# Fused block-causal attention and a routed expert layer: moving the gate products, the routing steps and the scatters of the records within the attention slots

## The chip, the cores and the metric

The kernel runs on one core of a Trainium2 chip. The core has a matrix engine (TensorE, here PE; its weight loads are shown apart as PEld), VectorE (DVE), ScalarE (ACT), GpSimd (POOL) and SyncE (SP), which issues most DMA transfers. The metric is the device time of the one launch in microseconds (us), given as the median of several runs.

## What is computed

```python
# attention: q, k, v are [8, 8, 576, 64] float32
scores = scale * np.matmul(q, k.transpose(0, 1, 3, 2))        # scale = 1/8
scores = np.where(block_i >= block_j, scores, -1e9)           # blocks of 64
scores = scores - np.max(scores, axis=-1, keepdims=True)
attn = np.exp(scores)
attn = attn / (np.sum(attn, axis=-1, keepdims=True) + 1e-09)
attn_out = np.matmul(attn, v)

# routed layer: x is [4608, 512], one row a token
x = attn_out.transpose(0, 2, 1, 3).reshape(B * S, H * D)
logits = x @ w_gate + modality_bias[modality_id]              # 8 experts
e_idx = np.argmax(logits, axis=1)
gate_w = softmax(logits)[np.arange(N), e_idx]
for e in range(E):
    h = np.maximum(x[mask] @ w1[e], 0.0)                      # mask = (e_idx == e)
    out[mask] = gate_w[mask, None] * (h @ w2[e])              # inner width 1024
```

## The kernel before

**Tiling.** The 64 pairs of batch and head are taken two heads at a time: 32 pairs, four to a batch (`PPB`). One pair fills the 128 partitions, head 0 on the lower 64 and head 1 on the upper 64. The 576 positions are nine blocks of 64; block row s needs the scores against blocks 0 to s.

**Stages of a pair**, one letter each in the order table, and the engine:

- `Q` (POOL, line 203; `A` on ACT from pair 18 on) scales q in the tile `raw`, which `L` and `l` load over SP's queue. `v`, `v1`, `v2` load the values, `Y` loads `vt`, the values turned for the gates. A queue's transfers go in the order of issue, and a transfer waits for its buffer.
- `S0` to `S3`: the scores (PE, line 223, 40 matmul rows, shape 64\*64) into PSUM banks 0 to 5 (4 and 5 are one tile, `wide`).
- `M0` to `M4`: the maxima of the score rows (DVE, line 232), nine a pair; `E0` to `E4`: the exponentials (ACT) into `pm`, in the units of `UNITS`.
- `T0` to `T2`: transposes of 64 x 128 pieces of `pm` (PE, line 270, 16 + 16 + 14 pieces, two heads each; shape 64\*128), back into the same banks.
- `C0` to `C4`: copies of the transposed banks to `pt` (line 284). `ON_DVE` names those on DVE, here copy 1 alone; the rest are on ACT.
- `G`: the gate columns, v times the gate's weights (PE, line 290, 24 rows, shape 128\*64) into bank `b0` from column `GATES` on; `H` (ACT) copies them beside the values, so that the value product gives the logits of the gate along with the output.
- `V`: the value product (PE, line 312) into `o0` and `b0`: first 20 rows for the odd blocks (`TAILS`, 64 deep, shape 64\*64, the "short blocks"), then 80 rows, shape 128\*64 (`PRODUCTS`). [...]
- `D`, `Z0`, `Z1`: the reciprocal of the sums (DVE, lines 327 and 328) and the rows (DVE, lines 340 and 341): products and gate logits are divided into the token records `xr` and into `gl`. After these the banks `o0` and `b0` are free.

**Slots.** There is no loop on the chip: the program is laid out in 32 slots, and `run_slot` walks the table `ORDER` once per slot. Each entry is a stage and a distance: in slot n an entry with distance d works on pair n - d. So one slot loads pair n + 2, scores pair n + 1, transposes and copies pair n, and multiplies pair n - 1. The order is by hand; each engine works its instructions strictly in that order. The gates of pair n stand between its transposes and the scores of pair n + 1.

**Routing.** When the four pairs of a batch are through (`Z1` of pair 3, 7, ...), `routing` adds 20 small steps to a list: logits, total (PE, line 365), its copy out, bias, maximum, hits, index, first, one-hot, counts (PE, lines 406 and 408), shift, exponential, copy out of the counts, weight, running, and five that find the place of each token in its expert's list. The entries `q1` to `q6` of the order take up to 4 (`q1`) or 2 steps; total and counts are taken at `qp` only, their copies at `qv`. A batch's steps stretch over some three slots. The last one writes the indices `pi` (line 437) and queues nine **scatters** (line 440: an indirect DMA, issued by POOL, which writes the 128 records of a block row to their places in `records`, 77824 rows of 272 numbers in HBM). One scatter is issued at each of the spots `SPOTS` = V, T2, M1 of a slot.

**Experts.** From slot 19 on POOL also splits the first expert's weights into a high and a low part (lines 643 and 644, the step "prep" in `EARLY_STEPS`), loaded by the steps "stage". The last value product and the last scatters lie inside the first expert products (table `LAST`). Then two matmuls per token tile and expert run to the end of the program.

## Time and profile before

| | |
|---|---|
| runs | 707.65, 708.3, 709.89 us; median 708.3 |
| profiled execution | 709.1 us, of it the span of the trace 707.2 |
| PE | 688.3 us busy (97%), granted clock 0.996 over the span |
| PE weight loads | 577.6 us (82%) |
| DVE | 341.1 us (48%) |
| ACT | 327.4 us (46%) |
| POOL | 209.5 us (30%) |

A slot's start is where its first short block's product begins. Sums by stretch show one slot beside another, timelines show single instructions and, behind them in brackets, how long the engine had stood idle and what released it; "issue" means that the trace shows nothing for which it waited. Neighbouring instructions on PE overlap in such rows, so what a row of products takes is read from one start to the next, not from its duration.

### The profile page before, as it was taken

How to read it: one execution, taken by the hardware profiler on the slowest of the kernel's cores; microseconds unless marked ns; L12 is line 12 of the kernel's file. 1: busy time of each engine (PE TensorE's matmuls, PEld its weight loads, DVE VectorE, ACT ScalarE, POOL GpSimd, SP SyncE). 2: the span in 40 equal slices, each digit the busy share in tenths (PEclk: the TensorE clock that was granted, in tenths of full speed). 3: DMA queues.
4: the chain of work that ended last, by engine and by line, in shares of the span. 5: the costliest groups of instructions: out<-in, count | busy, mean ns of one | idle time of the engine just before them, and what ended most of it. 6: DMA issues, size and time to landing. Idle time of an engine off the chain costs nothing. (4 is left out here: it accounts for less than half of the span.)

```text
span 707.2 us, 21037 instructions
## 1 busy us (share of the span) xinstructions
PE 688.3 (97%) x8647; PEld 577.6 (82%) x8647; DVE 341.1 (48%) x929; ACT 327.4 (46%) x654; POOL 209.5 (30%) x246
## 2 busy tenths in 40 slices
PE   8999999989999999999999999999999999999996
PEld 5887887878788888888888888888888888888894
DVE  5786776868697878574132421424113142232121
ACT  6886776768787879432131321313113032231221
POOL 2424445250648583669012020301002010020201
PEclk9999999999999999999999999999999999999999
DMA  7555555565787787504842141501707031020100
GB/s 232 158 161 163 172 168 173 158 182 151 238 221 235 229 247 209 134 33 150 152 89 91 25 96 60 119 1 33 204 1 227 11 56 65 1 82 1 61 28 22
DMA packets 68451, 85.48 MB, mean 121 GB/s; under 512 B 12350, under 2 KB 54782, under 8 KB 68352
## 3 DMA queue, kind: packets, MB, share of 16 engines
q1 hardware_dynamic: 61824, 64.59, 34.7%
q0 software_dynamic: 6528, 19.50, 7.6%
q8 instruction: 69, 1.13, 0.7%
q14 instruction: 30, 0.25, 0.1%
HBM read 62.97 MB, written 21.27 MB: 119 GB/s over the span
## 5 line engine op out<-in xcount | busy, mean ns | idle before, releaser
L802 DVE SCALAR_TENSOR_TENSOR extra<-bank,extra 128x512 fp32r<-128x512 f32 (+1 forms) x70 | 46.8, 669 | 242.7 <-ACT extra L801 242.7
L801 ACT ACTIVATE extra<-bank 128x512 fp32r<-128x512 f32 (+1 forms) x70 | 40.6, 580 | 215.3 <-PE bank L798 215.3
L312 PE MATMUL b<-v,pt 64*64 64x73 f32 (+1 forms) x1612 | 103.4, 228 | 4.8 <-issue 4.7
L241 ACT ACTIVATE pm<-bank,nm 128x64 f32<-128x64 f32 (+3 forms) x192 | 88.0, 531 | 33.4 <-DVE nm L232 32.0
L232 DVE TENSOR_REDUCE nm<-bank 128x1 f32<-128x64 f32 (+3 forms) x192 | 80.6, 482 | 42.0 <-PE bank L223 32.3
L440 POOL DMA_INDIRECT records<-xr,pi x72 | 73.5, 1020 | 90.9 <-DVE pt L284 41.7
L312 PE MATMUL o<-v,pt 64*64 64x73 f32 (+1 forms) x1488 | 96.4, 230 | 2.3 <-issue 2.3
L312 PEld LDWEIGHTS o<-v,pt 64*64 64x64 f32 (+1 forms) x1488 | 82.1, 137 | 16.4 <-issue 11.0
L312 PEld LDWEIGHTS b<-v,pt 64*64 64x64 f32 (+1 forms) x1612 | 87.0, 137 | 7.1 <-issue 6.5
L223 PE MATMUL bank<-raw 64*64 64x448 f32 (+5 forms) x768 | 88.8, 441 | 0.0
L223 PE MATMUL wide<-raw 64*64 64x128 f32 (+3 forms) x512 | 59.9, 369 | 1.3 <-ACT pm L241 0.9
L284 ACT COPY pt<-bank 128x512 f32<-128x512 f32 x95 | 49.7, 594 | 20.5 <-PE bank L270 19.6
L798 PE MATMUL bank<-extra,w0ha 128*128 128x512 f32 (+1 forms) x176 | 59.2, 362 | 0.0
L798 PE MATMUL bank<-extra,w0la 128*128 128x512 f32 (+1 forms) x152 | 56.6, 372 | 0.0
L915 POOL DMA_INDIRECT out<-scratch,ids_b x9 | 8.8, 974 | 155.1 <-ACT scratch L914 154.2
L223 PEld LDWEIGHTS bank<-raw 64*64 64x64 f32 x768 | 40.9, 133 | 13.8 <-issue 6.9
L907 PE MATMUL late<-extra 128*128 128x512 f32 x216 | 50.4, 389 | 0.0
L798 PE MATMUL bank<-xtl,w0ha 128*128 128x512 f32 x128 | 49.8, 389 | 0.0
L798 PE MATMUL bank<-extra,w0hb 128*128 128x512 f32 x128 | 49.8, 389 | 0.0
L798 PE MATMUL bank<-extra,w0lb 128*128 128x512 f32 x128 | 49.8, 389 | 0.0
L798 PE MATMUL bank<-xtl,w0hb 128*128 128x512 f32 x128 | 49.8, 389 | 0.0
L241 ACT ACTIVATE pm<-wide,nm 128x128 f32<-128x128 f32 (+2 forms) x96 | 43.8, 526 | 10.8 <-DVE nm L232 8.1
(239 smaller groups left out, 1230.0 us busy)
## 6 DMA issues: line engine op xcount, KB each, us to landing
vt<-qk SPq DMA_DIRECT2D x32, 288.0 KB
v<-vr SPq DMA_DIRECT2D x62, 146.0 KB
xr<-records SPq DMA_DIRECT2D x32, 256.0 KB
raw<-qk SPq DMA_DIRECT2D x30, 240.0 KB
raw<-qk SPq DMA_DIRECT2D x30, 192.0 KB
raw<-qk SPq DMA_DIRECT2D x30, 144.0 KB
staging<-w SPq DMA_DIRECT2D x32, 128.0 KB
v<-vr SPq DMA_DIRECT2D x31, 73.0 KB
```

What stands on the lines that cost most here:

```text
L223: pe.matmul(place(s, a, b)[64 * t : 64 * t + 64], d.q[hs, D * s : D * s + D], d.k[hs, a:b], start=True, stop=True)
L232: dve.tensor_reduce(pairs[p].nm[:, s : s + 1], whole(s), AX.X, ALU.max, negate=True)
L241: act.activation(d.pm[:, o : o + D * (s + 1)], whole(s), AF.Exp, bias=d.nm[:, s : s + 1], scale=1.0)
L284: dve.tensor_copy(dst, src) if c in (ON_DVE if p else FIRST_ON_DVE) else act.copy(dst, src)
L312: pe.matmul(o, d.pt[rows, at, t : t + 64], d.v[rows, block, h, :], start=key not in begun, stop=last)
L440: last = pool.indirect_dma_start(records[:], bass.IndirectOffsetOnAxis(ap=g.pi[:, i : i + 1], axis=0), xr[:, i, :], None, bounds_check=2 * ...
L798: nc.tensor.matmul(hp, w[:, kc, ms], x[:, kc, 0:n], start=i == 0, stop=i == len(mm) - 1)
L801: nc.scalar.activation(hh, hp, AF.Relu)
L802: nc.vector.scalar_tensor_tensor(hl, hp, 0.0, hh, ALU.max, ALU.subtract)
L907: nc.tensor.matmul(y, s.hs[m][x][:, ts], self.part(w, 1, m // 2)[:, m % 2, :], start=first, stop=last)
L915: last = nc.gpsimd.indirect_dma_start(self.out, bass.IndirectOffsetOnAxis(ap=s.list.ids[:, s.t + i : s.t + i + 1], axis=0), yo, None, boun ...
```

## The change

- `V` is split: `tails` (V) multiplies the short blocks, `values` (W) the rest. Between them now stand the gates of the next pair (`G`) and the entry `qm`, at which total and counts are taken. Since the short blocks have by then started the banks, gates, total and counts no longer start them (`start` is false, but for pair 0 and the last batch).
- Order within the slot: the loads of `vt` (`Y`) come ahead of the values' (`v1`, `v2`); on DVE the copies come ahead of the rows `Z0`, `Z1`; transposes go T0, T2, T1, and blocks are regrouped among banks and transposes (`UNITS`, `GROUPS`, `ROOMS`, `PIECES`, `FLIP`) with the same number of rows. Slot 0 has an order of its own.
- Copy 2 is on DVE too, except for the last pair of a batch and for the six pairs of `BUSY`.
- `q9`, ahead of the scores and maxima, takes up to six routing steps in slots 13 and 29 (`QUICK`); the other entries take other numbers of steps.
- Scatters go at T2 and M1, at V too only in slots with slot % 4 == 1; in slots 30 and 31 at five spots.
- "stage1" and "restage" move from `qp` to `v1`, "ids" from slot 21 to 24, and the opening of pair 0 interleaves maxima and exponentials in another way.

```diff
...
-UNITS = ((7,), (5, 0), (4, 2), (6,), (3, 1, 8))
+UNITS = ((7,), (4, 2), (5, 0), (3, 1, 8), (6,))
...
-FLIP = (5, 0, 3, 1, 8)
-PIECES = (((7, 0, 512),), ((5, 0, 384), (0, 0, 64)), ((4, 0, 320), (3, 0, 256), (1, 0, 128), (2, 0, 192)), ((8, 512, 576), (8, 0, 512), (6, 0, 448)))
+FLIP = (4, 2, 3, 1, 8)
+PIECES = (((7, 0, 512),), ((4, 0, 320), (2, 0, 192)), ((8, 0, 512), (5, 0, 384), (0, 0, 64)), ((6, 0, 448), (8, 512, 576), (3, 0, 256), (1, 0, 128)))
...
-ON_DVE, FIRST_ON_DVE = (1,), (1, 3)
+ON_DVE, FEW_ON_DVE, FIRST_ON_DVE = (1, 2), (1,), (1, 2, 3)
+BUSY = (13, 14, 15, 16, 29, 30)
...
-ORDER = (
-    ("Q", -1), ("L", -2), ("V", 1), ("v", -1), ("l", -2), ("v1", -1), ("v2", -1), ("D", 1), ("Z0", 1), ("Z1", 1), ("q1", 1), ("T0", 0), ("C0", 0), ("C1", 0), ("T1", 0), ("C2", 0), ("C3", 0),
-    ("T2", 0), ("C4", 0), ("G", 0), ("H", 0), ("Y", -1), ("qp", 1), ("q2", 1), ("q3", 1), ("q4", 1), ("qv", 1), ("A", -2), ("S0", -1), ("S1", -1), ("S2", -1), ("S3", -1), ("M0", -1), ("E0", -1), ("M1", -1), ("E1", -1), ("M2", -1), ("E2", -1),
+BEGIN = (("Q", -1), ("L", -2), ("V", 1), ("G", 0), ("qm", 1), ("W", 1), ("v", -1), ("l", -2), ("Y", -1), ("v1", -1), ("v2", -1), ("D", 1), ("T0", 0), ("C0", 0))
+END = (
+    ("qp", 1), ("q2", 1), ("H", 0), ("qv", 1), ("q9", 1), ("A", -2), ("S0", -1), ("S1", -1), ("S2", -1), ("S3", -1), ("M0", -1), ("E0", -1), ("M1", -1), ("E1", -1), ("M2", -1), ("E2", -1),
     ("M3", -1), ("E3", -1), ("M4", -1), ("E4", -1), ("q5", 1), ("q6", 1),
 )
+FIRST_ORDER = (*BEGIN, ("C1", 0), ("T1", 0), ("C2", 0), ("C3", 0), ("T2", 0), ("C4", 0), *END)
+ORDER = (*BEGIN, ("C1", 0), ("T2", 0), ("C4", 0), ("T1", 0), ("C2", 0), ("C3", 0), ("Z0", 1), ("Z1", 1), ("q1", 1), *END)
...
-OPENING = (((0, 2, 1, 3), ((0,),)), ((6, 5, 4, 7), ((2,), (1, 3))), ((8,), ((5,), (6,), (4,), (7,), (8,))))
...
+OPENING = (("s", 0), ("p", 0, 2, 1, 3), ("m", 0), ("s", 1), ("m", 2), ("e", 0, 2), ("p", 5, 6, 4, 7), ("m", 1, 3), ("e", 1, 3), ("p", 8), ("m", 5), ("e", 5), ("m", 6), ("e", 6), ("m", 4), ("e", 4), ("m", 7), ("e", 7), ("m", 8), ("e", 8))
...
+SPOTS, LATE_SPOTS = ("V", "T2", "M1"), ("V", "T2", "S0", "M1", "M4")
 EARLY_STEPS = {
     **{(slot, name): ("prep",) for slot in range(19, 30) for name in SPOTS if (slot, name) != (29, "M1")},
-    (18, "V"): ("chosen",), (18, "qp"): ("stage",), (19, "qp"): ("stage1",), **{(slot, "qp"): ("restage",) for slot in range(20, 31)}, (31, "qp"): ("restage1",), **{(slot, "v2"): ("more",) for slot in range(19, 32)}, (21, "L"): ("ids",), (26, "T0"): ("fetch",), (31, "T0"): ("fetch",), (30, "S0"): ("turn0",), (31, "V"): ("low0", "low0"),
+    (18, "V"): ("chosen",), (18, "qp"): ("stage",), (19, "v1"): ("stage1",), **{(slot, "v1"): ("restage",) for slot in range(20, 31)}, (31, "v1"): ("restage1",), **{(slot, "v2"): ("more",) for slot in range(19, 32)}, (24, "L"): ("ids",), (26, "T0"): ("fetch",), (31, "T0"): ("fetch",), (30, "S0"): ("turn0",), (31, "V"): ("low0", "low0"),
...
...
-        dve.tensor_copy(dst, src) if c in (ON_DVE if p else FIRST_ON_DVE) else act.copy(dst, src)
+        dve.tensor_copy(dst, src) if c in (FIRST_ON_DVE if not p else FEW_ON_DVE if p % PPB == PPB - 1 or p in BUSY else ON_DVE) else act.copy(dst, src)
...
-                pe.matmul(b0[64 * c : 64 * c + 64, o : o + 2 * NE], vt[:, at : at + 64], wg[:, p % PPB, :], start=True, stop=True)
+                pe.matmul(b0[64 * c : 64 * c + 64, o : o + 2 * NE], vt[:, at : at + 64], wg[:, p % PPB, :], start=not p, stop=not p)
...
+    def product(p, s, block, at, rows, last):
+        d = pairs[p]
+        bank, c = column(p, s)
+        for h in range(2):
+            t = 64 * (h ^ (s in FLIP))
+            o = bank[t : t + 64, VW * c : VW * c + VW]
+            key = (s in SUMS[0], t)
+            pe.matmul(o, d.pt[rows, at, t : t + 64], d.v[rows, block, h, :], start=key not in d.begun, stop=last)
+            d.begun.add(key)
+
+    def tails(p):
+        pairs[p].begun = set()
+        for s, block, at, upper in TAILS:
+            product(p, s, block, at, slice(64 * upper, 64 * upper + 64), False)
+        assert len(pairs[p].begun) == 4
...
-        for s, block, at, upper in TAILS:
-            product(s, block, at, slice(64 * upper, 64 * upper + 64), False)
         for n, ((s,), j) in enumerate(PRODUCTS):
             side = SUMS[s not in SUMS[0]]
-            product(s, j, POS[s, j], slice(0, 128), all(x[0] not in side for x, _ in PRODUCTS[n + 1 :]))
+            product(p, s, j, POS[s, j], slice(0, 128), all(x[0] not in side for x, _ in PRODUCTS[n + 1 :]))
...
-                pe.matmul(tot[c], ii[:, c], g.l0, start=True, stop=True)
+                pe.matmul(tot[c], ii[:, c], g.l0, start=b == B - 1, stop=b == B - 1)
...
-                pe.matmul(ps[c, 0 : NSUB * NE].rearrange("p (e c) -> p c e", e=NE), ones[:, c], ohe.rearrange("p (c e) -> p c e", e=NE), start=True, stop=True)
+                pe.matmul(ps[c, 0 : NSUB * NE].rearrange("p (e c) -> p c e", e=NE), ones[:, c], ohe.rearrange("p (c e) -> p c e", e=NE), start=b == B - 1, stop=b == B - 1)
             for c in (slice(0, 64), slice(64, 128)):
-                pe.matmul(ps[c, NSUB * NE :], lead[:, c], ohe, start=True, stop=True)
+                pe.matmul(ps[c, NSUB * NE :], lead[:, c], ohe, start=b == B - 1, stop=b == B - 1)
...
-        total.kind = counts.kind = "qp"
+        total.kind = counts.kind = "qm"
...
     def run_slot(slot):
         nonlocal steps, ex
-        for name, stage in LAST if slot == NPAIR else ORDER:
+        for name, stage in LAST if slot == NPAIR else ORDER if slot else FIRST_ORDER:
             p = slot - stage
-            if placing and slot < NPAIR and name in SPOTS:
+            if placing and slot < NPAIR and name in (LATE_SPOTS if slot >= NPAIR - 2 else SPOTS[slot % PPB != 1 :]):
...
-                for _ in range(1 if kind else 4 if name == "q1" else 2):
+                chosen = steps and getattr(steps[0], "kind", "") == "c"
+                if kind:
+                    most = 1
+                elif name == "q9":
+                    most = 6 * (slot in QUICK)
+                elif name == "q1":
+                    most = 3 if chosen else 4
+                elif name == "q2":
+                    most = 2 * (not chosen)
+                else:
+                    most = 4 if chosen or slot % PPB == PPB - 1 or slot - 1 in QUICK else 2
+                for _ in range(most):
                     if slot > 1 and steps and getattr(steps[0], "kind", "") in kinds:
                         steps.pop(0)()
                 continue
```

**PE, a slot in which a batch's total is taken** (pair 7 multiplies, pair 8 is transposed; `cf` with `pm` is a transpose, `raw` a score, `wg` a gate, `l` the total, `v` with `pt` a value product). Before:

```order
L270 MATMUL bank_98<-cf,pm_111 128x64
L270 MATMUL wide<-cf,pm_111 128x64 x14
L290 MATMUL b_100<-wg,vt 64x16 x12
L365 MATMUL o_99<-l_886,cf 64x72 x2
L223 MATMUL bank_95<-raw_107 64x512 x2
L223 MATMUL bank_97<-raw_107 64x384 x2
```

After:

```order
L311 MATMUL b_100<-v_109,pt_113 64x73 x2
L311 MATMUL o_99<-v_109,pt_113 64x73 x2
L292 MATMUL b_100<-wg,vt 64x16 x12
L369 MATMUL o_99<-l_950,cf 64x72 x2
L311 MATMUL o_99<-v_109,pt_113 64x73 x2
L311 MATMUL b_100<-v_109,pt_113 64x73 x2
```

Gates and total stood between the last transposes and the first scores; now they stand between the short blocks (64x73, the first rows of `v` with `pt`) and the rest of the value product, whose rows the program names in the same way. Transposes are followed by scores.

**DVE, a slot with routing steps of batch 1**, from the reciprocal to the first maxima (`den`, `inv`: the reciprocal; COPY `pt`: copies 1 and 2; `xr`, `gl`: the rows; `ix`, `oh`: routing; `nm`: maxima). Before:


**DVE, the slot in which the one-hot of batch 0 is made** (`den`, `inv`: the reciprocal; COPY `pt`: copies 1 and 2; `xr`, `gl`: the rows; `ix`, `oh`, `df`: routing; `nm`: maxima). Before:

```order
L328 RECIPROCAL inv<-den 128x9
L340 TENSOR_TENSOR xr_79<-b_100,inv 128x5x64
L341 TENSOR_TENSOR gl<-b_100,inv 128x40
L340 TENSOR_TENSOR xr_79<-o_99,inv 128x4x64
L341 TENSOR_TENSOR gl<-o_99,inv 128x32
L397 TENSOR_REDUCE ix<-eq 128x9
L401 TENSOR_TENSOR oh<-cf,ix 128x72
L284 COPY pt_114<-bank_96 128x2x4x64
L384 TENSOR_TENSOR df<-lg,mx 128x72
L232 TENSOR_REDUCE nm<-bank_95 128x1
```

After:

```order
L332 RECIPROCAL inv<-den 128x9
L286 COPY pt_113<-bank_96 128x2x4x64
L286 COPY pt_113<-bank_97 128x8x64
L344 TENSOR_TENSOR xr_79<-b_100,inv 128x5x64
L345 TENSOR_TENSOR gl<-b_100,inv 128x40
L344 TENSOR_TENSOR xr_79<-o_99,inv 128x4x64
L345 TENSOR_TENSOR gl<-o_99,inv 128x32
L401 TENSOR_REDUCE ix<-eq 128x9
L405 TENSOR_TENSOR oh<-cf,ix 128x72
L236 TENSOR_REDUCE nm<-bank_95 128x1
L236 TENSOR_REDUCE nm<-bank_96 128x1 x2
```

The copies stand ahead of the rows, copy 2 is new on DVE, and the slot is the one before (its copies go to the other tile `pt`): the counts, which take `oh`, now come at `qm` of the next slot.

**POOL, the scatters of batch 0** (DMA `records`, x2 for two in a row; `raw`: the scale `Q`; `xr` from `cf`: the token numbers of the next batch). Before:

```order
L203 TENSOR_SCALAR raw_107<-raw_107 128x576
L440 DMA records<-xr_105,pi 77824x272 x2
L203 TENSOR_SCALAR raw_106<-raw_106 128x576
L440 DMA records<-xr_105,pi 77824x272 x3
L203 TENSOR_SCALAR raw_107<-raw_107 128x576
L440 DMA records<-xr_105,pi 77824x272
L354 TENSOR_SCALAR xr_79<-cf 128x9
L440 DMA records<-xr_105,pi 77824x272 x2
L203 TENSOR_SCALAR raw_106<-raw_106 128x576
L440 DMA records<-xr_105,pi 77824x272
L203 TENSOR_SCALAR raw_107<-raw_107 128x576
```

After:

```order
L207 TENSOR_SCALAR raw_107<-raw_107 128x576
L444 DMA records<-xr_105,pi 77824x272
L358 TENSOR_SCALAR xr_79<-cf 128x9
L444 DMA records<-xr_105,pi 77824x272
L207 TENSOR_SCALAR raw_106<-raw_106 128x576
L444 DMA records<-xr_105,pi 77824x272 x3
L207 TENSOR_SCALAR raw_107<-raw_107 128x576
L444 DMA records<-xr_105,pi 77824x272 x2
L207 TENSOR_SCALAR raw_106<-raw_106 128x576
L444 DMA records<-xr_105,pi 77824x272 x2
L207 TENSOR_SCALAR raw_107<-raw_107 128x576
```

Before, the nine stood as 2, 3, 1, 2, 1 between the scales; now the first comes a scale later and they stand as 1, 1, 3, 2, 2. Behind the last weight conversions, later in the queue, POOL now has five scatters of batch 5 and five of batch 6 in a row; before, five of batch 6 alone.

## Rows read from the trace of the kernel before

**Rows 1.** The page's first part: busy us (share of the span) xinstructions.

```profile
PE 688.3 (97%) x8647; PEld 577.6 (82%) x8647; DVE 341.1 (48%) x929; ACT 327.4 (46%) x654; POOL 209.5 (30%) x246
```

**Rows 2.** Sums by stretch: length, busy us (instructions) by engine, clock, DMA share, GB/s.

```profile
93.37:101.47 8.10, 8.10 (x215) 7.18 (x210) 7.30 (x28) 6.62 (x15) 1.38 (x2) 1.00 0.58 159
101.47:113.91 12.44, 10.61 (x215) 8.35 (x208) 5.34 (x16) 7.00 (x15) 10.28 (x10) 1.00 0.53 163
139.19:152.36 13.17, 11.10 (x214) 8.43 (x207) 7.22 (x34) 7.38 (x15) 11.22 (x11) 1.00 0.55 168
177.72:188.51 10.79, 9.59 (x214) 7.79 (x210) 6.19 (x19) 7.57 (x17) 7.63 (x11) 1.00 0.75 214
250.01:258.94 8.93, 8.73 (x215) 7.48 (x211) 5.92 (x19) 7.51 (x17) 7.95 (x12) 1.00 0.85 259
284.55:294.97 10.42, 8.71 (x174) 7.54 (x167) 6.26 (x18) 5.62 (x13) 6.14 (x6) 0.84 0.72 166
294.97:702.00 407.03, 406.88 (x1968) 339.15 (x1964) 123.11 (x231) 101.67 (x170) 73.51 (x79) 1.00 0.26 70
```

**Rows 3.** Timeline of PE around the gates: start us, us, instruction, shape, count, idle before.

```profile
90.00 0.88 PE L290 MATMUL b<-wg,vt 128*64 128x16 f32 x24
90.72 0.24 PE L406 MATMUL o<-oh,ones 128*64 128x72 bf16 x2
...
96.61 1.21 PE L270 MATMUL bank<-cf,pm 64*128 64x64 f32 x32
97.66 0.60 PE L270 MATMUL wide<-cf,pm 64*128 64x64 f32 x14
98.19 0.88 PE L290 MATMUL b<-wg,vt 128*64 128x16 f32 x24
99.00 0.65 PE L223 MATMUL bank<-raw 64*64 64x512 f32 x4
```

**Rows 4.** Timeline of PE in slot 11, beside the scatters of rows 5.

```profile
101.65 0.52 PE L312 MATMUL o<-v,pt 64*64 64x73 f32 x4
102.54 0.30 PE L312 MATMUL b<-v,pt 64*64 64x73 f32 x2 [0.37 <-issue]
...
105.09 0.57 PE L312 MATMUL b<-v,pt 128*64 128x73 f32 x4
106.02 0.44 PE L312 MATMUL b<-v,pt 128*64 128x73 f32 x5 [0.37 <-issue]
106.80 0.36 PE L312 MATMUL b<-v,pt 128*64 128x73 f32 x3 [0.34 <-issue]
107.53 0.36 PE L270 MATMUL bank<-cf,pm 64*128 64x64 f32 x5 [0.38 <-issue]
108.28 0.90 PE L270 MATMUL bank<-cf,pm 64*128 64x64 f32 x22 [0.38 <-issue]
```

**Rows 5.** Timeline of POOL, single scatters and a scale.

```profile
99.78 1.02 POOL L440 DMA_INDIRECT records<-xr,pi  x1 [8.64 <-DVE pt L284]
101.11 0.98 POOL L440 DMA_INDIRECT records<-xr,pi  x1 [0.30 <-issue]
...
118.57 1.66 POOL L203 TENSOR_SCALAR raw<-raw 128x576 f32<-128x576 f32 x1 [5.16 <-DMA raw<-qk]
...
282.36 1.00 POOL L440 DMA_INDIRECT records<-xr,pi  x1 [11.40 <-DVE pi L437]
...
288.03 1.47 POOL L440 DMA_INDIRECT records<-xr,pi  x1 [0.30 <-issue]
```

**Rows 6.** What gates (L290) and counts (L406) waited for: us, times.

```profile
  DVE gl L341: 1.9, 6
...
  DVE oh L401: 0.4, 1
```

**Rows 7.** Timeline of DVE: first and last of four row instructions, and the copy.

```profile
88.99 0.49 DVE L340 TENSOR_TENSOR xr<-b,inv 128x320 f32<-128x320 f32 x1
...
89.83 0.20 DVE L341 TENSOR_TENSOR gl<-o,inv 128x32 f32<-128x32 f32 x1
...
90.33 0.68 DVE L284 COPY pt<-bank 128x512 f32<-128x512 f32 x1
```

More of the change, by code (lines that the diff above doesn't have):

```diff
@@ L39 @@
 NWARM = 7
+QUICK = (13, 29)
 FIRST = 256
@@ L86 @@
 }
 LAST = (
-    ("+up0", 0), ("+place", 0), ("V", 1), ("+place", 0), ("D", 1), ("Z0", 1), ("Z1", 1), ("+steps1", 0), ("+place", 0), ("+up1", 0),
+    ("+up0", 0), ("+place", 0), ("V", 1), ("W", 1), ("+place", 0), ("D", 1), ("Z0", 1), ("Z1", 1), ("+steps1", 0), ("+place", 0), ("+up1", 0),
     ("+place", 0), ("+steps8", 0), ("+place", 0), ("+up2", 0), ("+place", 0), ("+steps11", 0), ("+up3", 0), ("+flush", 0),
@@ L243, in exps @@
     def exps(p, u):
-        for s in UNITS[u]:
+        for s in (8, 3, 1) if u == 3 else UNITS[u]:
             exp(p, s)
@@ L249, in opening @@
         pairs[0].nm = sml.tile([128, NSUB], F32, name="nm")
-        for n, (products, rows) in enumerate(OPENING):
-            if n < 2:
-                part = q[:, n * FIRST : FIRST if n == 0 else S]
-                dve.tensor_scalar(part, part, SCALE, None, ALU.mult)
-            for s in products:
-                for a, b in ((512, 576), (0, 512)) if s == 8 else ((0, D * (s + 1)),):
-                    score(0, s, a, b)
-            for together in rows:
-                for s in together:
-                    maximum(0, s)
-                for s in together:
-                    exp(0, s)
+        for what, *items in OPENING:
+            for s in items:
+                if what == "s":
+                    part = q[:, 0:FIRST] if s == 0 else q[:, FIRST:S]
+                    dve.tensor_scalar(part, part, SCALE, None, ALU.mult)
+                elif what == "p":
+                    for a, b in ((512, 576), (0, 512)) if s == 8 else ((0, D * (s + 1)),):
+                        score(0, s, a, b)
+                else:
+                    (maximum if what == "m" else exp)(0, s)
     def transposes(p, g):
@@ L300, in column @@
         return sides(p)[k], SUMS[k].index(s)
-    def values(p):
-        d = pairs[p]
-        begun = set()
-        def product(s, block, at, rows, last):
-            bank, c = column(p, s)
-            for h in range(2):
-                t = 64 * (h ^ (s in FLIP))
-                o = bank[t : t + 64, VW * c : VW * c + VW]
-                key = (s in SUMS[0], t)
-                pe.matmul(o, d.pt[rows, at, t : t + 64], d.v[rows, block, h, :], start=key not in begun, stop=last)
-                begun.add(key)
-        for s, block, at, upper in TAILS:
-            product(s, block, at, slice(64 * upper, 64 * upper + 64), False)
+    def product(p, s, block, at, rows, last):
[12 more added lines that the diff above has]
+        assert len(pairs[p].begun) == 4
+    def values(p):
         for n, ((s,), j) in enumerate(PRODUCTS):
             side = SUMS[s not in SUMS[0]]
-            product(s, j, POS[s, j], slice(0, 128), all(x[0] not in side for x, _ in PRODUCTS[n + 1 :]))
+            product(p, s, j, POS[s, j], slice(0, 128), all(x[0] not in side for x, _ in PRODUCTS[n + 1 :]))
     def inverse(p):
@@ L496, in emit @@
         one = {
-            "L": lambda: load(p), "Q": lambda: scale(p), "A": lambda: scale_late(p), "V": lambda: values(p), "D": lambda: inverse(p), "G": lambda: gates(p), "H": lambda: gates_out(p), "Y": lambda: load_turned(p),
+            "L": lambda: load(p), "Q": lambda: scale(p), "A": lambda: scale_late(p), "V": lambda: tails(p), "W": lambda: values(p), "D": lambda: inverse(p), "G": lambda: gates(p), "H": lambda: gates_out(p), "Y": lambda: load_turned(p),
             "v": lambda: load_blocks(p, 4, 6, slice(64, 128)), "l": lambda: load_part(p, QK_PARTS[2:]), "v1": lambda: load_blocks(p, 0, 2), "v2": lambda: load_blocks(p, 2, 4),
```

8 lines of the change are left out of this document (4 added, 4 removed), and 6 rows, old and new, of the table GROUPS.

## The prediction

> **What bounds the kernel now.** I read the page first, then the sums by stretch, then the timelines of TensorE (PE) and GpSimd (POOL). PE is busy 97% of the span and no other engine half of it [rows 1]; the last 407 us, the experts' products, are PE without a gap at full clock [rows 2]. Nothing in them is edited, so they move as a block, and the question is what the 32 attention slots take, 295 us. A slot is one pass over the order table. An undisturbed slot takes 8.10 us, and PE and its weight loads fill it [rows 2]. Others with the same 214 or 215 matmul rows take 12.44, 13.17, 10.79 and 8.93 us [rows 2]. I compared every slot's start with the next (the first products of the short blocks mark it): together the 31 slots lose about 31 us against the undisturbed one, and they lose it in three ways.
>
> First, **changes of the matmul's shape**. The gates stand between transposes (64*128) and scores (64*64), themselves 128*64. Followed by scores, 24 gate rows take 0.81 us (98.19 to 99.00); followed by counts of their own shape, 0.72 (90.00 to 90.72) [rows 3]. So gate to score costs 0.09. The last 14 transposes take 0.53 before a gate; at the pace of the 32 ahead of them (1.05, so 0.033 each) they would take 0.46: 0.07 more [rows 3].
>
> Second, **runs of scatters**. In slots 7, 8, 11, 12, 15, 16, 19 and 31 PE stands still with "issue" as the only releaser, each time while POOL issues scatters back to back, 1.0 us each and 0.3 apart [rows 4, 5]. Of two in a row whose first lies on scores, the second (101.11 [rows 5]) makes the four rows at 101.65 take 0.89 us to the next instead of some 0.1: 0.8 lost [rows 4]. For three in a row, the 17 rows from 105.09 to 108.28 should take 0.54 us at the 0.032 of a gate row or a transpose, and take 3.19: 2.65 lost [rows 4]. Four singles in a slot, with other POOL work between them, go with 8.93 instead of 8.10: 0.2 each [rows 2]. [...] Why PE is held I cannot say from these rows; that it is held I can.
>
> Third, **waits of the gates and counts for VectorE (DVE)**: 1.9 us in six slots for the logits of the pair before, 0.4 for the one-hot [rows 6].
>
> **The change, part by part.**
>
> *Gates, totals and counts move between the short blocks and the values' product.* No matmul goes. The shape change from short blocks to value products is there anyway; the gates now take it, and value products follow in the gates' own shape. Gone are the two changes around the old place, 0.09 + 0.07; new is the step from transposes straight to scores, which no row shows. Bounds: nothing, or the whole 0.16. The nearest rows are the two single changes, so 0.08. The gain is 0.08 x 31 = **2.5 us**, between 0 and 5.0. [...]
>
> *The gates' waits.* At the new place the gates write a bank that the short blocks ahead of them needed free already, and the counts' one-hot is made a slot earlier. Both waits go: **2.3 us**. What is late next is below.
>
> *Scatters.* The first scatter of a batch used to stand in POOL's queue behind one scale, some 9 us before its indices were ready (8.64 us idle at 99.78 [rows 5]), and the scale behind it came late, so three, then three more ran in a row. Now the last routing step ends a slot before the first scatter is met, and the rest goes two a slot, three in one slot of four, each behind that slot's scale, which waits for its load (118.57 [rows 5]). By batch, with the prices above:
> - Batches 0 and 1: runs of 2 (another POOL step between, so half a pair's price), 3, 2, 2, so 0.4 + 2.65 + 0.8 + 0.8 = 4.65 each. Before: slot 11 lost 4.3 [rows 2] and, by the starts of the slots, slot 12 0.4, slots 7 and 8 4.5 + 0.6. Gain 0.5.
> - Batch 2: after the last scale on POOL nothing paces it, so six follow each other; 1.1 x 6 - 0.7 = 5.9 in small products, 4.9 if the first falls on scores. Before: 5.1 (slot 15 [rows 2]) and, in the slot behind it, 0.7. Gain 0.9.
> - Batch 3: singles, spaced by weight conversions, 0.2 each, so 1.8. Before: 2.7 in slot 19 [rows 2] and 0.4 behind it. Gain 1.3. Batch 4: unchanged.
> - Batch 5: now 4 singles and, once the conversions are done, a run of five, whose first and part of the second lie on scores: 0.8 + 4.8 - 1.3. Before: 0.8 in each of two slots, 1.6. Loss 2.7.
> - Batch 6: five in a row as before, but its indices come in the transposes of slot 31 instead of before its products, so most of the run lies beside the first expert products (4.8 matmul rows per us in that stretch against 26 in a slot [rows 2]). What reaches the last value products I put at 1.4; before 4.8. Gain 3.4.
>
> Sum **3.4 us**; from +5 (runs at the full price everywhere) to -9 (most of them hidden by scores).
>
> *Copies and rows on DVE and ScalarE (ACT).* One 128x512 copy a slot goes from ACT (about 0.6) to DVE (0.68 [rows 7]) in 19 slots, and the rows (four instructions, 88.99 to 90.03 [rows 7]) go behind the copies. Set on a slot's clock with the transposes starting at 0: den and reciprocal, which stand ahead of the rows now too, to about 0.5, first copy 0.80 to 1.48, second 1.75 to 2.43, rows to 3.4, maxima 3.4 to 7.1 (the rest of DVE's 5.92 in a slot without routing [rows 2]), with 8.0 for the slot. The scores begin when the 46 transposes are through, at 1.55, and take their banks over the next 1.6 us; the copies end between 1.4 and 2.7: in time. The next short blocks start 2.47 behind the first score, at 4.0, and need the rows done at 3.4; before, that slack was some 3 us, now it is 0.6. Routing adds up to 2.0 us in one slot of four, the one that keeps its copy on ACT. I charge **1.0 us**; bounds 0 and 7. Loads of vt move ahead of the value loads on SyncE's queue; they wait for the gates, which now end 2.5 us before the value products that the loads behind them wait for anyway. The opening's new order of exponentials keeps its products and maxima; nothing, give or take 0.5.
>
> **Sum.** -2.5 - 2.3 - 3.4 + 1.0 = -7.2 us. The profiled execution took 709.1 (span 707.2 and 1.9 around it), 0.8 above the median of 708.3, so 701.9 there and about **701.0** as a median.
>
> **The rivals.**
> - *Scatters cost what they cost before*: 709.1 - 0.8 - 2.5 - 2.3 + 1.0 = 704.5. For it: the number of scatters is the same, and new runs of six and five take the place of threes. Against: the price is paid per run, not per scatter only. [...]
> - *No change*: the runs pay the full price, 1.5 for each pair, 5.9 for six, 4.8 for both fives; together about 5 more than before. 708.3 - 3.8 + 5 = 709.5.
> - *More*: the step from transposes to scores is free (-2.5) and the pairs hide beside scores (-4): 694.5.
> - *Slower: DVE sets the period.* Place: the short blocks' wait for the rows of the slot before. DVE's own work in an undisturbed slot with routing is 7.30 [rows 2]; with 0.68 more and the two waits for transposes that the new order puts inside (0.27 each) it is 8.5, against 8.0 for PE. It decides as soon as DVE is over 0.6 late at the rows. Price: 8.5 - 8.1 in two slots of three, 20 x 0.4 = 8, no gain from the shape changes since PE then waits; scatter runs still cost theirs: 708.3 - 2.3 - 3.4 + 8 = 710.6. Against: a slot without routing has 5.92 [rows 2], so late work can be caught up, and the slot with the most routing keeps its copy on ACT.
>
> **How the numbers follow.** Forecast 701.0 (699 to 703): 0.40. Scatters as before, 704.5: 0.18. More, 694.5: 0.14. No change, 709.5 (706.2 to 710.4): 0.15. Slower, 710.6 and up: 0.13. A measurement of this kernel tells about 0.3%, 2.1 us, from none. Faster by more: 0.40 + 0.18 + 0.14 = 0.72; within: 0.15; slower: 0.13. The range leaves a tenth out at each end: 692 to 710.
>
> **What would show it.** Gates followed by value products with no step, and an undisturbed slot near 8.0 (first part; 7.9 means the new step is free). No idle time of a gate on `gl`. Scatter runs of 2, 3, 2, 2 on POOL, six around slot 16, two fives at the end, with "issue" gaps of the sizes above; slot 31 without its 4.8 us. It is wrong if short blocks wait for DVE, if scores wait for copies, or if a pair of scatters costs as much as three did.

## The result and the profile after

The changed kernel takes 718.9 us (717.6 to 720.5) where the one before takes 708.3: a ratio of 1.0146, 95% interval 1.0124 to 1.0168, so 10.6 us slower where 7.3 faster was forecast. One thing has to be known ahead of all that follows: the unchanged kernel before took 707.9 to 712.8 us in some of the sets of runs below and 682.5 to 683.9 in others, and in the traces of the latter PE does not stop beside scatters (slot 16 of the changed kernel, beside a run of six, takes 8.16 us in a_third below and 16.63 in the trace of this section); so each figure is read against the kernel before in its own set, and I call the sets **stopping** (the two traces of before and after are of that kind) and **free**.

The page of the changed kernel, its span, its busy times (as in [rows 1]) and the clock granted in 40 slices of the span:

```profile
span 718.5 us, 20950 instructions
...
PE 694.8 (97%) x8647; PEld 578.3 (80%) x8647; DVE 350.1 (49%) x948; ACT 318.5 (44%) x635; POOL 208.4 (29%) x246
...
PEclk9999999989999998899999999999999999999999
```

The work is the same (8647 matmuls), and the span is 11.3 longer. Three slices have a lower clock; before had none. The sums by stretch of the changed kernel, with the columns of [rows 2], show where: slots 8, 9, 16, 29 and 30, then the experts from slot 32's start on.

```profile
71.31:80.86 9.55, 9.26 (x216) 7.19 (x212) 7.18 (x27) 5.71 (x12) 4.89 (x5) 1.00 0.53 163
80.86:94.00 13.14, 11.00 (x217) 9.38 (x212) 6.79 (x20) 6.52 (x15) 5.92 (x6) 0.87 0.50 152
151.52:168.15 16.63, 12.03 (x217) 9.68 (x213) 7.55 (x31) 6.99 (x16) 5.79 (x6) 0.79 0.44 131
271.95:286.96 15.01, 11.56 (x225) 8.55 (x221) 7.58 (x25) 7.50 (x16) 9.94 (x13) 0.85 0.55 175
286.96:297.94 10.98, 10.98 (x219) 9.85 (x216) 6.94 (x21) 7.55 (x18) 0.00 (x0) 0.74 0.45 130
308.15:715.00 406.85, 404.33 (x1941) 336.55 (x1940) 122.82 (x230) 100.93 (x168) 76.88 (x83) 1.00 0.26 71
```

Slots 7, 11, 15, 19 and 31 of the kernel before lost 4.5, 4.3, 5.1, 2.7 and 4.8; here they are cured, and slot 16 alone takes 16.63, slot 29 15.01. In slot 30 not one scatter stands, and it is 1.8 us longer than the same slot in a free set (9.18, below), at 0.74 of the clock.

What stands in slot 16: the timeline of POOL (start us, us, instruction, idle before), the run of six behind which nothing paces it.

```profile
151.32 1.06 POOL L444 DMA_INDIRECT records<-xr,pi  x1 [0.27 <-issue]
152.69 0.98 POOL L444 DMA_INDIRECT records<-xr,pi  x1 [0.30 <-issue]
...
157.85 0.98 POOL L444 DMA_INDIRECT records<-xr,pi  x1 [0.30 <-issue]
```

The timeline of PE beside it, gate rows (L292) and value products (L311):

```profile
155.63 0.27 PE L292 MATMUL b<-wg,vt 128*64 128x16 f32 x2 [0.52 <-issue]
157.04 0.54 PE L311 MATMUL o<-v,pt 128*64 128x73 f32 x4 [1.14 <-issue]
157.76 0.28 PE L311 MATMUL b<-v,pt 128*64 128x73 f32 x1 [0.19 <-issue]
158.63 0.39 PE L311 MATMUL b<-v,pt 128*64 128x73 f32 x2 [0.59 <-issue]
...
160.04 0.52 PE L311 MATMUL o<-v,pt 128*64 128x73 f32 x4 [0.43 <-issue]
```

And the sums in steps of 2 us through the slot:

```profile
152.00:154.00 2.00, 1.11 (x19) 0.85 (x16) 1.50 (x6) 1.21 (x4) 1.39 (x3) 1.00 0.33 87
156.00:158.00 2.00, 0.78 (x5) 0.30 (x4) 0.00 (x0) 0.00 (x0) 1.39 (x3) 0.55 0.32 111
158.00:160.00 2.00, 0.71 (x4) 0.31 (x3) 0.00 (x0) 0.00 (x0) 0.83 (x1) 0.50 0.79 242
160.00:162.00 2.00, 1.96 (x32) 1.97 (x34) 0.00 (x0) 0.00 (x0) 0.00 (x0) 0.50 0.42 106
162.00:164.00 2.00, 2.00 (x48) 1.92 (x46) 0.16 (x1) 0.00 (x0) 0.00 (x0) 0.75 0.15 59
164.00:166.00 2.00, 2.00 (x54) 1.78 (x56) 1.65 (x6) 1.31 (x3) 0.00 (x0) 1.00 0.56 150
```

PE works 4 or 5 rows in 2 us instead of some 53 (54 from 164 to 166). Its clock then falls to 0.50 and is still there when the scatters are over and PE is busy again: 32 rows from 160 to 162. The run costs twice, once while it stands and once at the lower level behind it.

### The profile page after: what moved, and what is told of

The parts are those of the page before. It is cut to its first block, busy times and chain, and to the rows that moved or that the text cites. A ratio compares the mean times of both kernels' runs of the same rounds, so it can differ in the third digit from the quotient of the medians.

```text
span 718.5 us, 20950 instructions
## 1 busy us (share of the span) xinstructions
PE 694.8 (97%) x8647; PEld 578.3 (80%) x8647; DVE 350.1 (49%) x948; ACT 318.5 (44%) x635; POOL 208.4 (29%) x246
## 5 line engine op out<-in xcount | busy, mean ns | idle before, releaser
L311 PE MATMUL b<-v,pt 64*64 64x73 f32 (+1 forms) x1612 | 101.9, 232 | 1.3 <-issue 1.3
L311 PE MATMUL o<-v,pt 64*64 64x73 f32 (+1 forms) x1488 | 98.9, 234 | 1.9 <-issue 1.8
L245 ACT ACTIVATE pm<-bank,nm 128x64 f32<-128x64 f32 (+3 forms) x192 | 90.7, 537 | 21.2 <-DVE nm L236 19.1
L227 PE MATMUL bank<-raw 64*64 64x64 f32 (+5 forms) x768 | 92.6, 448 | 3.0 <-issue 2.0
L311 PEld LDWEIGHTS b<-v,pt 64*64 64x64 f32 (+1 forms) x1612 | 87.3, 141 | 1.9 <-issue 1.5
L311 PEld LDWEIGHTS o<-v,pt 64*64 64x64 f32 (+1 forms) x1488 | 84.7, 142 | 3.7 <-issue 3.1
L227 PE MATMUL wide<-raw 64*64 64x128 f32 (+3 forms) x512 | 62.3, 375 | 2.2 <-issue 1.9
L227 PEld LDWEIGHTS bank<-raw 64*64 64x64 f32 x768 | 37.3, 135 | 33.3 <-issue 15.9
L286 ACT COPY pt<-bank 128x512 f32<-128x512 f32 x76 | 43.7, 595 | 42.7 <-PE bank L272 33.7
L207 POOL TENSOR_SCALAR raw<-raw 128x576 f32<-128x576 f32 x17 | 28.2, 1657 | 77.5 <-DMA raw<-qk 48.2
```

The costliest lines, as they stand in the source:

```text
L207: pool.tensor_scalar(d.q, d.q, SCALE, None, ALU.mult)
L227: pe.matmul(place(s, a, b)[64 * t : 64 * t + 64], d.q[hs, D * s : D * s + D], d.k[hs, a:b], start=True, stop=True)
L245: act.activation(d.pm[:, o : o + D * (s + 1)], whole(s), AF.Exp, bias=d.nm[:, s : s + 1], scale=1.0)
L286: dve.tensor_copy(dst, src) if c in (FIRST_ON_DVE if not p else FEW_ON_DVE if p % PPB == PPB - 1 or p in BUSY else ON_DVE) else act.copy(d ...
L311: pe.matmul(o, d.pt[rows, at, t : t + 64], d.v[rows, block, h, :], start=key not in d.begun, stop=last)
```

## The experiments

Undisturbed pieces of a slot are read from one start on PE to the next. Before, in slots without scatters: short blocks 0.47 to 0.54, values 2.70, transposes 1.57, gates 0.72 (0.81 with the step to scores), scores 2.45 to 2.52.

**The gates alone** (e_gates): the kernel before, with one line of the table and its helpers changed.

```diff
-("V", 1), ("v", -1), ("l", -2)
+("V", 1), ("G", 0), ("W", 1), ("v", -1), ("l", -2)
...
-("T2", 0), ("C4", 0), ("G", 0), ("H", 0)
+("T2", 0), ("C4", 0), ("H", 0)
```

> The kernel before with one part of the change alone: the 24 gate rows stand between the short blocks and the rest of the value product; totals, counts, scatters, copies and rows stay. Theory A (the gates are not what made the changed kernel slow; the scatters are): by the forecast's own price, 0.08 us in each of 31 slots and 1.9 us of waits, 708.3 - 4.4 = 703.9, and no slower than 708 in any case. Theory B (the gates' old place was slack that the copies of the transposes need, 0.8 us a slot): scores wait for copies in most slots, 708.3 + 3 or more.

735.6 against 708.8 in its set: 1.0356 (1.0315 to 1.0397), 27 us slower. Theory B holds in its time; its reason holds for half of the slots. In a slot with no scatter and no routing product the scores follow the transposes at once and take 3.12 to 3.17 instead of some 2.5; a timeline of PE shows the step (38.95 to 40.60) that they wait in:

```profile
38.42 0.60 PE L270 MATMUL wide<-cf,pm 64*128 64x64 f32 x14
38.95 1.61 PE L223 MATMUL bank<-raw 64*64 64x512 f32 x16
40.60 0.43 PE L223 MATMUL wide<-raw 64*64 64x256 f32 x2
```

In a slot with a total or counts these still stand behind the transposes, and they wait for DVE: in slot 4 the transposes and the wait behind them take 2.24 for 1.57, and the scores 2.48. What scores (L223) and, in the second view, the total (L367) wait for over the program (us, times; in the kernel before the scores wait 0.9 for these copies and the total nothing):

```profile
  ACT pt L284: 7.3, 18
  DVE pt L284: 0.7, 4
```

```profile
  DVE l L363: 10.7, 14
```

So the gates at their old place covered two things, 0.5 to 0.7 us a slot: the copies of the transposed banks, and DVE's logits and one-hot. The change moves total and counts too, which this run does not, and has a new order of transposes, banks and copies; the forecast had no term for either cover. That the new order is what keeps the move from costing this much is likely, but no run takes it alone.

**Copy 2 back on ACT** (e_c2act).

```diff
-ON_DVE, FEW_ON_DVE, FIRST_ON_DVE = (1, 2), (1,), (1, 2, 3)
+ON_DVE, FEW_ON_DVE, FIRST_ON_DVE = (1,), (1,), (1, 2, 3)
```

> The changed kernel with copy 2 of every pair back on ACT. Theory D (VectorE's longer slot is what made the change slow: it was priced as a rival at 8 us): 711, within 2. Theory A (scatters made it slow): VectorE has room, the time stays at 718.9 within 2; ACT's copies 2 and 3 then stand behind each other, so it may be 1 to 2 us slower.

718.3 against 708.8 (1.0143, 1.0108 to 1.0177): the same as the changed kernel. VectorE's longer slot is not the cause; theory D falls. One thing shows in the slots without scatters: with copy 2 on ACT the scores take 2.68 or 2.69 in all of them (slots 2 to 7, 17 and 18) where the changed kernel, which has it on DVE in most, takes 2.48 in slots 4 to 6, 17 and 18.

**Where a pair of scatters stands** (e_scores, e_products, e_place and p_again, which is e_place in another set). The spots are replaced by one small copy on POOL that waits for a tile, and two scatters behind it (three in one slot of four):

```diff
+            if placing and 0 < slot < NPAIR and name == "S0":
+                pool.tensor_copy(held, pairs[slot].pt[:, POS[5, 2], 64:65])
+                for _ in range({NPAIR - 2: 4, NPAIR - 1: 5}.get(slot, 3 if slot % PPB == 1 else 2)):
```

e_products has `"V"` and `pairs[slot].nm[:, 6:7]` there, e_place `"S0"` and `pairs[slot].pt[:, 0, 0:1]`.

> The changed kernel (718.9), but the scatters are issued two a slot (three in one slot of four, four in slot 30, five in slot 31) behind one small copy on POOL that waits for the last transposed copy of the slot, so that they run beside the scores. Theory P (a scatter's price hangs on the place: some 1.1 us beside small products, almost nothing beside scores, whose rows are long): only the thirds and the runs of slots 30 and 31 still cost, about 1 us each for 8 of them and 4 more; the 46 us that the slots lose fall to some 20: 693, within 4. Theory R (only the length of a run counts, as in the forecast): pairs at 0.8 in 24 slots and threes at 2.65 in 7, 38 lost: 711.

> The same as the run beside it that holds the scatters to the scores, with the same number in each slot, but the small copy waits for the last maximum of the slot before, so that the scatters run beside short blocks, gates and value products. Theory P (place): 1.0 us or so for each of 63 scatters, some 60 lost where the changed kernel loses 46: 730, within 6. Theory R (only the run's length): the same time as its neighbour, within 3 us.

> The changed kernel with the scatters held as in the run that held them to the last transposed copy, but behind the first transposed copy of the slot, some 1.3 us earlier, so that a pair starts about 6.1 and 7.4 us into the slot, beside the scores; same numbers per slot (two, three in one slot of four, four in slot 30, five in 31). Theory P (place decides: pairs there cost nothing, as in three slots of the changed kernel and four of the one before; a third falls into the next slot's small products and costs about 1): slots lose about 15 instead of 46: 688, within 6. Theory R (a pair costs the same 1.6 wherever it stands, as the two runs that held them elsewhere showed): 738, within 5.

> The changed kernel with pairs of scatters held behind the first transposed copy, as in the run of that name, on another chip if before is near 708. Theory P (beside scores a pair is free also on a chip where scatters stop PE; a third costs 1; the last expert part is 5 us longer, as it was): 694, within 5. Theory R (1.6 a pair wherever it stands): 738, within 6. With before near 682 it repeats its 689.5.

e_scores took 745.0 and e_products 739.0 against 708.8: both far slower, and neither put the scatters where I meant to. The timelines of POOL show it: a scatter starts 0.58 behind the end of so small a copy, and the maximum comes later than I thought, so that in e_scores most pairs began 9.1 to 9.6 us into a slot, with the second some 1.0 into the next, beside gates, and in e_products stood mostly near 4.2 and 5.6, beside transposes; either cost 1.6 to 1.7 a pair. e_place ran in a free set (689.5 against 682.5, 6 us of it a longer expert part: 415.3 for 409.2) and told nothing of P. p_again, in a stopping one, took 723.0 against 712.8: 29 above P's 694, 15 below R's 738. Its first pair stands at 6.24 and 7.67 of slot 8. That slot takes 7.96 as without scatters, but the second scatter (79.03 to 80.02) lies over the start of slot 9, whose short blocks take 1.43 for 0.55:

```profile
79.03 0.99 POOL L445 DMA_INDIRECT records<-xr,pi  x1 [0.30 <-issue]
```

```profile
80.38 0.22 PE L312 MATMUL o<-v,pt 64*64 64x73 f32 x1 [0.39 <-issue]
```

So the first scatter of the pair is free and the second costs 0.9; the pairs behind it, at some 7.1 and 8.5, cost 0.7 to 0.9 in the same way, the threes 1 to 4. The expectation says that such pairs cost nothing in "four of the one before"; they do not: behind the pairs of slots 6, 10 and 14 there the next slot's short blocks take 1.48, 1.40 and 1.38 for 0.53, much as the prediction had it (0.8). A pair that stands wholly beside scores, in slot 10 of the changed kernel (5.87 and 7.20), costs less: the short blocks behind it take 0.82 for 0.55. So place matters, as P says, but I could not hold the pairs there, and as a forecast P failed.

**The table of scatters alone** (b_two, t_again the same in another set; b_place and bp_again hold pairs in the kernel before as above, behind its copy 3):

```diff
-            if placing and slot < NPAIR and name in SPOTS:
+            if placing and slot < NPAIR and name in (LATE_SPOTS if slot >= NPAIR - 2 else SPOTS[slot % PPB != 1 :]):
...
-(21, "L"): ("ids",)
+(24, "L"): ("ids",)
```

> The kernel before with only the changed kernel's table of scatters (two a slot, a third one in slots with slot % 4 == 1, five spots in slots 30 and 31) and the first list's slot that goes with it (24 for 21); routing steps, gates, copies and rows stay. By the forecast's prices for runs: 3 or so faster, 705. By what the changed kernel showed (runs of five and six cost 8 to 10 us with what the clock takes afterwards): this table alone makes most of the 10 us, 714 to 722.

> The kernel before with the changed kernel's table of scatters alone, again. With before near 708: by the forecast's prices 705; by the changed kernel's own trace (runs of five and six cost 8 to 10 us each) 714 to 722. With before near 682 it repeats 682.

> The kernel before with its scatters held behind its third transposed copy on ACT, two a slot, three in one of four, four in slot 30, five in 31, so that pairs start about 6.4 and 7.7 us into the slot; nothing else is changed but the slot in which the first list is read (24 for 21). Theory P: pairs are free there, thirds cost about 1, the last nine about 5: the slots lose 15 to 18 instead of 35: 690, within 5. Theory R: 1.6 a pair and 2.6 a three, 48 lost: 721.

> The kernel before with pairs of scatters held to the scores, again. With before near 682 it repeats 689. With before near 708: Theory P (a pair beside scores is free, a third costs 1 or more): 700, within 6. Theory N: 725.

b_two: 682.0 against 682.5, free, no difference. t_again: 717.6 against 712.8 (1.0063, 1.0043 to 1.0083), where the forecast's prices said 3 faster and the changed kernel's trace 6 to 14 slower. So the table by itself costs 4.8 us in a stopping set and nothing in a free one; that is more than half of the 8.0 that the whole change loses in the same set (a_again, below); what the rest comes from, the earlier routing steps or the missing cover of the copies, these two do not part. b_place and bp_again (689.0 and 689.4, both in free sets) show only the longer expert part and leave P open in the kernel before.

**The changed kernel itself, again** (a_again, a_third).

> The changed kernel itself, unedited. The kernel before took 708.3 and 708.8 us on two chips and 682.5 on a third, where the trace of a variant shows no stop of PE beside scatters at all. Theory S (the scatters, where they stop PE, are the whole loss of the change): on a chip with before near 708 this takes 718.9 again; on one with before near 682 it takes 682 within 2, since gates, copies and rows give and take less than 1 us. Theory O (the new order of gates, copies and rows costs something by itself): on such a chip 687 or more.

> The changed kernel itself, unedited, beside the two paced ones. With before near 708: 719 to 721 again. With before near 682: if the scatters, where they stop PE, are the whole loss of the change, 683 within 2, since the two paced kernels, with and without the change's gates, copies and rows, were within 0.3 us of each other; if the new order costs something by itself, 687 or more.

a_again: 720.8 against 712.8 (1.0101, 1.0063 to 1.0138). a_third, in a free set: 682.3 against 682.8, ratio 0.9983 (0.9969 to 0.9998). With nothing stopping PE the change gains 0.1 to 2.1 us. Theory S holds: the loss is there only where the scatters stop PE. How much a single run of scatters takes differs from one execution to the next: a_again has 14.08 in slot 13 for 12.50, and 13.00 and 9.34 in slots 29 and 30 for 15.01 and 10.98, both at a clock of 1.00. The slots 16, 29 and 30 of a_third, the same program with the same runs of scatters:

```profile
137.49:145.65 8.16, 8.16 (x216) 7.19 (x212) 7.49 (x31) 6.99 (x16) 5.95 (x6) 1.00 0.82 257
245.32:253.65 8.33, 8.33 (x223) 7.27 (x217) 6.32 (x20) 7.27 (x16) 7.20 (x10) 1.00 0.79 246
253.65:262.83 9.18, 8.53 (x221) 7.36 (x217) 8.97 (x27) 7.44 (x18) 2.94 (x3) 1.00 0.84 220
```

**One multiplication ahead of each scatter** (a_pace on the changed kernel, b_pace on b_two; three sets each).

```diff
+                if (slot, name) not in EARLY_STEPS or "prep" not in EARLY_STEPS[slot, name]:
+                    pool.tensor_scalar(rest_of, rest_of, 1.0, None, ALU.mult)
                 g, c = placing.pop(0)
                 g(c)
```

> The changed kernel, same places in the order, but ahead of each scatter in a slot POOL works one 128x448 multiplication on a tile of its own (about 1.3 us), unless weight conversions stand there already, so that no two scatters stand back to back. Theory B (what stops PE is the row of scatters back to back; single ones 2.4 us apart cost about 0.25 each, as in the slots with conversions): the runs of five, six and three are gone, 718.9 - 25 = 694, within 6. Theory N (each scatter costs about 0.6 wherever and however it stands): no gain, 719, within 3. Where before takes near 682, no theory sees a difference: 683.

> The kernel before with the changed kernel's table of scatters and the same multiplication ahead of each; it leaves gates, copies, rows and routing as they were. Theory B: the slots lose 63 x 0.25 and what is left at the end, 18 instead of 30 to 35: 695, within 5, and faster than both kernels. Theory N: 709 or more. Against its neighbour of the changed kernel it tells what gates, copies and rows are worth without runs of scatters: the forecast says the neighbour is 3.8 faster; the runs in which nothing stopped PE say the same within 2.

> The changed kernel with one multiplication on POOL ahead of each scatter, a second time, because in its first set of runs (before: 683.9) nothing stopped PE beside scatters. With before near 708: Theory B (the row back to back is what stops PE): 694, within 6. Theory N (each scatter costs the same however it stands): 719, within 3. With before near 682: 684 again.

> The kernel before with the changed kernel's table of scatters and the same multiplication ahead of each, a second time for the same reason. With before near 708: Theory B: 695, within 5. Theory N: 709 or more. With before near 682: 684 again.

> The changed kernel with one multiplication on POOL ahead of each scatter, a third time: its first two sets of runs were ones in which scatters stop nothing. With before near 708: Theory B (the row back to back is what stops PE): 694, within 6. Theory N (each scatter costs the same however it stands): 719, within 3. With before near 682: 684 again.

> The kernel before with the changed kernel's table of scatters and the same multiplication ahead of each, a third time for the same reason. With before near 708: Theory B: 695, within 5. Theory N: 709 or more. With before near 682: 684 again.

In two free sets all four are level with before (684.4 and 684.1 against 683.9; 683.4 and 683.1 against 682.8). In the third, a stopping one, a_pace took 698.4 against 707.9 (0.9884, 0.9837 to 0.9931) and b_pace 697.8 (0.9865, 0.9830 to 0.9901). Theory B holds for both, in the upper half of its ranges (694 and 695 were the middles): with POOL work of 1.3 us between two scatters the changed kernel is 17 to 20 us faster than without, each read against before in its own set (9.5 faster, where it was 8.0 and 10.6 slower). The two differ by 0.2, 0.3 and 0.6 us in the three sets, so without runs of scatters the change's gates, copies, rows and opening are together worth nothing that these runs can tell. The same run of batch 2 on POOL, and slot 16, in a_pace3:

```profile
148.45 1.03 POOL L446 DMA_INDIRECT records<-xr,pi  x1 [0.18 <-issue]
149.51 1.35 POOL L548 TENSOR_SCALAR rest_of<-rest_of 128x448 f32<-128x448 f32 x1
151.04 1.02 POOL L446 DMA_INDIRECT records<-xr,pi  x1 [0.17 <-issue]
```

```profile
143.12:152.89 9.77, 9.28 (x216) 7.41 (x212) 9.16 (x33) 7.35 (x16) 9.01 (x9) 1.00 0.62 189
```

9.77 where the unpaced slot took 16.63, with three scatters in it, at full clock. What is left, 698.4 against some 684 for the same kernel in free sets, is 14 us for 57 scatters in the slots: 0.25 each on the average. These two are the fastest kernels of the study in a stopping set, and no slower than before in a free one.

## Why the prediction was wrong

**The scatters' term failed: -3.4 forecast, +8 to +11 measured.** What they cost each kernel is its time in a stopping set less that in a free one: before 708.3 - 682.8 = 25.5, the changed kernel 718.9 - 682.3 = 36.6, so 11 more; in the set of a_again it is 712.8 - 682.8 = 30.0 and 720.8 - 682.3 = 38.5, so 8.5 more. By slots, the changed kernel against a_third:
- Batches 0 and 1, forecast 4.65 each: 1.6 + 5.0 (slots 8 and 9) and 1.6 + 3.9 + 1.3 (slots 12 to 14), so 13.4 for 9.3.
- Batch 2, 4.9 to 5.9: 8.5 (slot 16).
- Batch 5, 0.8 + 3.5: 0.1 + 6.7 + 1.8 (slots 28 to 30), 8.6 for 4.3.
- Singles between conversions, and batch 6's run at slot 31: close to the forecast (4.0 in slots 19 to 27; 0.5 in slot 31 and 1.2 behind it, for 1.4).

The 5.9 and 4.9 for six in a row and the 1.3 off a five that starts on scores are terms that no run shows: they are my estimates, from a law of 1.1n - 0.7 for n in a row, drawn through the 2.65 of three and the 4.8 of the five in slot 31 of the kernel before (10.42 us [rows 2], where 8.10 without the 2.47 of scores, from 99.00 [rows 3] to 101.47, would be 5.63). The runs showed 2.7 for the three of slot 9 (2.65 by the law) and 7.0 for the six of slot 16 up to 160.04, so for the time in which PE stands the law was not far off. Three things around it were missing. First, **the clock behind a run**. In slot 31 of the kernel before it is 0.84 [rows 2]; the 4.8 of that run of five has it inside, and I had no term for it behind any other. Here the runs end in dense products: the last 72 value rows of slot 16 take 3.85 us (160.04 to 163.89) where they take 2.4, so 1.45; slot 30 loses 1.8 without a scatter in it; the values of slot 9, behind a run of three, take 4.09 for 2.67 (a stretch of them below, 38 rows in 2 us). That is 4.6 us.

```profile
86.00:88.00 2.00, 2.00 (x38) 2.00 (x37) 0.00 (x0) 0.00 (x0) 1.79 (x2) 0.52 0.77 238
```

Second, **"started on scores" does not help a long run**: in slot 29 five of them make the scores last 8.51 for 2.69, 5.8 lost where I had 3.5; PE stops there too:

```profile
278.45 1.10 PE L227 MATMUL bank<-raw 64*64 64x512 f32 x12
281.46 1.08 PE L227 MATMUL wide<-raw 64*64 64x512 f32 x4 [1.91 <-issue]
284.07 1.65 PE L227 MATMUL bank<-raw 64*64 64x384 f32 x6 [1.53 <-issue]
```

Third, **a scatter beside the transposes makes the copies late**, and the gates no longer cover them. In slot 8 the last transposes start at 76.19 and the copy on DVE that follows them at 78.59, 2.4 later; in slot 6, without scatters, it is 59.94 and 60.71, so 0.8. The copy of slot 6, then the last transposes of slot 8 and the two copies that wait for them:

```profile
60.71 0.69 DVE L286 COPY pt<-bank 128x512 f32<-128x512 f32 x1 [0.21 <-PE bank L272]
```

```profile
76.19 0.66 PE L272 MATMUL bank<-cf,pm 64*128 64x64 f32 x16
78.59 0.69 DVE L286 COPY pt<-bank 128x512 f32<-128x512 f32 x1 [1.66 <-PE bank L227]
78.61 0.59 ACT L286 COPY pt<-bank 128x512 f32<-128x512 f32 x1 [0.67 <-PE bank L227]
```

DVE and ACT start together (78.59 and 78.61), 1.7 us after the last transposes ended by the trace (76.85), and both had been idle, waiting for PE. So I take it that what comes late is PE's signal that the transposes are done and neither engine's own work; no row shows the signal itself. (The rows name the scores, L227, as releaser because these had begun by then; a copy reads transposes only.)

Over the program the scores of the changed kernel (L227) wait for copies like this (us, times):

```profile
  ACT pt L286: 4.7, 12
  DVE pt L286: 4.4, 7
```

In a_third the same line waits 0.3 + 0.4 us, and before it was 0.9 (L223). "If scores wait for copies" was one of my signs of being wrong. So "the copies end in time" was right for a slot's own clock and wrong beside a scatter; the pairs of batches 0 and 1 at that place cost 1.6 where I had 0.4.

**Gates, waits, copies: -3.8 forecast, -0.1 to -2.1 measured** (a_third). The shape changes came out as forecast: undisturbed slots of a_third are near 8.0 (slots 6 and 18 take 7.99 and 8.00, in b_two 8.09 and 8.10), so 0.1 for my 0.08. The step from gates to scores is gone (0.09), the transposes take 1.58 ahead of scores for 1.57 ahead of gates, so the new step is as dear as the old one there, and the gates no longer wait for `gl`. Three things that I had at nothing or too low took it back:
- In the slots whose copy 2 stays on ACT (3, 7, 11, 13 and others) the scores take 2.63 to 2.69 for 2.48. By e_c2act this hangs on copy 2; the forecast had the copies in time either way.
- In slots 13 and 29 `q9` puts six routing steps ahead of the maxima. The exponentials come late, and the next slot's transposes, which wait for them, take 2.53 for 1.57 in slots 14 and 30: 1.9 us. My 1.0 for VectorE was for copies and rows (0 within 2 by e_c2act, as far as copy 2 goes), not for this. One such wait in a_third, and the sum of all (us, times; none in b_two):

```profile
259.01 0.65 PE L272 MATMUL wide<-cf,pm 64*128 64x64 f32 x14 [0.65 <-ACT pm L245]
```

```profile
  ACT pm L245: 3.3, 6
```

- The gates wait for `vt` in a_third, 1.7 us in four slots; I had its load at nothing.

The opening, which I had at nothing give or take 0.5, starts the first slot 1.3 earlier (13.71; 15.03 in b_two), and the slots together are 1.9 longer than b_two's; so what gain there is in a free set is the opening's.

**The rivals.** "No change" named the right mechanism, runs at the full price, and stopped at 709.5 because the clock and the copies were not in it. "Scatters cost what they cost before" fell, since they cost 8 to 11 us more, and "DVE sets the period", my only slower one, had the right side for a wrong reason.

**What stays open.** Why scatters back to back stop PE, and what makes a set free or stopping, no run here shows. It is not the chip alone: the record has chip 3 for the free set of b_two and, a few minutes later, for the stopping one of t_again and a_again. Within a set all executions of the unchanged kernel are of one kind (681.0 to 686.7 in free ones, 705.0 to 714.5 in stopping ones). Whether the time between scatters is what helps in a_pace, or the other instruction on POOL, is open too, since no run spaced them without one. And that a pair wholly beside the scores costs only 0.3 in a stopping set rests on single slots (slot 10 of the changed kernel and of a_again), not on a kernel.

## What to carry to other kernels

Count how many indirect DMAs stand back to back in POOL's queue once its own paced work has run out, and look at what PE does there and at its clock behind it; a harmless instruction of about their own length between them was worth 17 to 20 us here. A stage between two dependent ones may be the cover of another engine's work, as the gates were here (0.5 to 0.7 us a slot in e_gates): before moving it, ask what else is finished during it. And run the unchanged kernel beside every variant, since here its own time moved by up to 30 us, three times what the change did.

## What the runs showed of the hardware

- One program took 682.5 to 683.9 us in some sets of runs and 707.9 to 712.8 in others; in a free one the same run of six scatters left slot 16 at 8.16 us.
- After the runs of three, six and five scatters in slots 9, 16 and 29 of the changed kernel PE's granted clock fell to 0.5 and stayed near it for some 4, 3 and 9 us of work behind the run (84 to 88, 160 to 163 and 284 to 293); the three of slot 13 left it at 1.00 in the same trace, and so did runs of three in the kernel before [rows 2]. The same run need not do it each time: the five in slot 29 of a_again left it at 1.00 (over the whole span the clock is 0.990 there and 0.984 in the profiled execution of the changed kernel).
- Beside a scatter not only PE's own instructions are held: in slot 8 the copies behind the last transposes, on DVE and ACT alike, came 2.4 us after these had begun, in slot 6 without a scatter 0.8 on DVE.
- Of two scatters in a row of which the first lies on scores, the second, where it reached the next slot's short blocks, cost 0.7 to 1.0 us there (before and p_again).
- With 1.3 us of other POOL work between them, scatters cost about 0.25 us each (a_pace3 against the same kernel in free sets).
